# The first block's down products by seven products of 256 columns in six of eight groups, and forms loaded from the second group on

## The chip, the cores and the metric

The kernel runs on one core of one Trainium2 chip. TensorE (PE) multiplies, VectorE (DVE), ScalarE (ACT) and GpSimd (POOL) work on tiles, SyncE (SP) issues the DMAs. The metric is the device time of one execution in microseconds, the median of several runs.

## The reference

```python
def _attn_ref(q, k, v, lam):                 # decayed linear attention, blocks of 64 positions
    for b in range(nb):
        ...
        intra = np.einsum('bhic,bhjc->bhij', qb, kb) * Dmask[None]
        intra = np.einsum('bhij,bhjd->bhid', intra, vb)
        inter = np.einsum('bhid,bhde->bhie', qb * lam_pow[None], kv_state)
        out[:, :, sl] = intra + inter
        ...
def _moe_ref(x, w_in, w_out):                # x: 1536 x 512, w_in: 512 x 2048, w_out: 2048 x 512
    h = x @ w_in
    sp = np.where(h > 20.0, h, np.log1p(np.exp(np.minimum(h, 20.0))))
    g = h * np.tanh(sp)
    return g @ w_out
def _moe2_ref(x, w_in, w_out):
    h = x @ w_in
    r = np.maximum(h, 0.0)
    g = r * r
    return g @ w_out
```

The output is `_moe2_ref(_moe_ref(x))` with x the attention's 1536 tokens of 512 features, in float32.

## The kernel before

The 1536 tokens are three blocks of 512. After the attention (up to some 62 us) come two MLPs, L = 0 and 1, each in four groups g of 512 hidden features. Per group and block there is an up part (x times 512 columns of w_in) and a down part (the gated hidden values times 512 rows of w_out, summed over the groups). To keep float32, `mm3` (line 369) makes every product of two float32 values as three matmuls of a high and a low part; `split` (line 379) makes the parts: ACT copies the high one (names `..h`), DVE subtracts it for the low one (names `..l`).

Blocks 1 and 2 are multiplied as a pair (`up_pair`, `down_pair`): a product of 2 x 2 blocks by seven products, numbered 1 to 7, of sums and differences instead of eight. `sums` (line 668) makes the sums of a weight, `forms` the differences of x. In the down part the kept sums of the groups so far are copied into PSUM ahead of a product, which then adds to them, and copied out again behind it. Block 0 has its own seven products of 256 columns in the up part (`up_own`, line 780) in seven of the eight groups (OWN); its down part (`down`, line 1017) is plain: per group two outputs of four rows of 12 matmuls of 512 columns, seeded from and evicted to the two kept sums `ac`. PSUM holds four units of two banks; SBUF is cut into 51 units of 4 KB per partition (UNITS).

The forms of x, 14 tiles of 512 KB for the pair and 8 for block 0, are stored to DRAM (`store_form`, `own_forms`) and loaded again for each group from SPILL and HOME on (`load_form`, `own_back`), which frees their units between uses.

No engine's order is written out by hand. `Plan` takes every step with an engine, an assumed time, reads and writes, and a rank for TensorE; it runs them through a list scheduler with a limited number of units, 20 times with adjusted due times, and keeps the order that ends first. All engines, SP's queue too, then issue strictly in the order kept. Tile names carry L, g and the product: `gh0100` is the high part of the gated values of L0, g1, block 0, half 0.

Of the kernel before, what the change touches and what calls it, by code (L numbers as in the profile page):

```python
# [12 lines left out]
F32 = mybir.dt.float32  # L13
# [7 lines left out]
P = 128  # L21
# [3 lines left out]
CH = 128  # L25
# [19 lines left out]

UNITS = 51
DEBUG = None
SPILL = (2, 2)
HOME = (1, 2)
OWN = ((0, 1), (0, 2), (0, 3), (1, 0), (1, 1), (1, 2), (1, 3))  # L50
BACK = 9.0
SPARE = (6, 3)
AHEAD = 55.0
UP = tuple(-1919 + i for i in range(16))

# [255 lines left out]
def attention_mlps(ctx, tc, lam, qk, kv, w_in, w_out, w2_in, w2_out, out):  # L311
# [72 lines left out]

    def halves(v):
        return [(v, 0), (v, 1)]

# [392 lines left out]
    def up_own(L, g, rank, rest):  # L780

        w = 2 * CH
        back = g >= HOME[L]
        if back:
            own_back(L, g)
        one, two = Val(f"ua{L}{g}", "P"), Val(f"ub{L}{g}", "P")
        for v in (one, two):
            v.full = v.seeded = True
        a, b, f_, e = (one, 0), (one, 1), (two, 0), (two, 1)

        def bank(x):
# [73 lines left out]
        for u in range(2):  # L865
            hi, lo = Val(f"gh{L}{g}0{u}", dtype=F32R), Val(f"gl{L}{g}0{u}", dtype=F32R)
            g_hi[L, g, 0, u], g_lo[L, g, 0, u] = hi, lo
            split(hi, lo, h[u], halves(h[u]))

    g_hi, g_lo, h_raw = {}, {}, {}  # L870

# [6 lines left out]
    def gated(L, g, t, u, h, in_psum):  # L878

        name = f"{L}{g}{t}{u}"  # L880
        if L and not in_psum:
            op("DVE", 1.14, lambda: nc.vector.scalar_tensor_tensor(  # L882
                out=tl(h), in0=tl(h), scalar=0.0, in1=tl(h), op0=ALU.max, op1=ALU.mult), [(h, 0)], [(h, 0)], name=f"rs{name}")
        elif not in_psum:
            op("ACT", 0.96, lambda: nc.scalar.activation(out=tl(h), in_=tl(h), func=AF.Relu if L else AF.Mish),
               [(h, 0)], [(h, 0)], name=f"r{name}", table=None if L else "mish")
        if L and in_psum:
            op("ACT", 0.96, lambda: nc.scalar.activation(out=tl(h), in_=tl(h), func=AF.Square),
               [(h, 0)], [(h, 0)], name=f"sq{name}")
        if t:  # L890
            h_raw[L, g, t, u] = h
            return
        hi, lo = Val(f"gh{name}", dtype=F32R), Val(f"gl{name}", dtype=F32R)
        g_hi[L, g, t, u], g_lo[L, g, t, u] = hi, lo
        split(hi, lo, h, [(h, 0)])

    def take(L, g, t, u, src):
        h = Val(f"h{L}{g}{t}{u}")
# [114 lines left out]
        take(L, g, 2, 0, e)  # L1013

    accs = {}

    def down(L, g, t, rank, early=None):
        final = g == NG - 1
# [192 lines left out]
    for L in range(2):  # L1211
        for g in range(NG):
            if (L, g) != (0, 0):
                weights(L, g, 0, 0)
                weights(L, g, 0, 1)

            if (L, g) == (1, 0):
                own_forms(1)
            turned = (L, g) in TURNED
            own_up = (L, g) in OWN  # L1220
            first = turned and ranks()
            if own_up:
# [12 lines left out]
            if not g:  # L1235
                forms(L, halves)
            if not g and not L:
                own_forms(L)
            if (L, g) not in OWN:
                sums(L, g)  # L1240
            before = (L, g) in BEFORE and ranks()
            if (L, g) in SPLIT:
                opening, before = before, ranks()
                up_pair(L, g, opening, ranks())
            elif opened:
                up_pair(L, g, opened, ranks(), opens=OPENS) if OPENS else up_pair(L, g, ranks())
            elif own_up:
                up_pair(L, g, *((first, first, first if MIDDLE else between) if turned else (between, ranks())), parted=not turned)
            else:
                up_pair(L, g, first or ranks())  # L1250
            sums(L, g, 1)
            first = turned and ranks()
            early, rest = (ranks(), ranks()) if turned and SPREAD[L] else (None, None)
            down(L, g, 0, before or ranks(), early)
            down_pair(L, g, first or ranks(), rest, between if own_up and turned and MIDDLE else None)

    ordered = sorted((o for o in plan.ops if o.name in FIRST), key=lambda o: FIRST[o.name])
# [52 lines left out]
```

## Time and profile before

| | us |
|---|---|
| median of 3 runs | 533.87 (533.33 to 534.17) |
| the profiled execution | 533.92 |
| its span, first to last instruction | 531.9 |
| TensorE busy | 522.7 |
| DVE busy | 435.6 |
| ACT busy | 416.5 |
| DMA moved | 123.25 MB |

The profile is one execution, recorded by the hardware profiler. Busy time is the union of an engine's instructions. Matmuls overlap each other in their pipeline, so a row of 12 is read from the chain or the timeline, not as 12 times the mean of one. A wait is put down to what ended it.

### The profile page before, as it was taken

What the parts mean: (1) busy time and instruction counts of PE and PEld (TensorE: products, weight loads), DVE (VectorE), ACT (ScalarE), POOL (GpSimd) and SP (SyncE); (2) the same over time, 40 slices, a digit from 0 to 9 for tenths busy, and PEclk for the clock granted to TensorE, in tenths of its full rate; (3) what the DMA queues carried; (4) which work ended last, traced back from release to release, by engine and by line L of the source; (5) the groups of instructions that cost most, each with busy time, mean ns of one, the idle gap of its engine ahead of it and who ended that gap; (6) DMA issues with size and microseconds to landing.
All of it is one profiled execution on the core that took longest, in us unless ns stands there. A gap on an engine that the chain in (4) does not pass through costs nothing.

```text
span 531.9 us, 8778 instructions
## 1 busy us (share of the span) xinstructions
PE 522.7 (98%) x3470; PEld 458.0 (86%) x3470; DVE 435.6 (82%) x472; ACT 416.5 (78%) x482; POOL 32.3 (6%) x32
## 2 busy tenths in 40 slices
PE   8899999999999999999999999999999999999997
PEld 5798788898888988889888888998899888988996
DVE  6999999986796659986999997997897279985851
ACT  3858478889999999968988995889797689858711
POOL 3575200000000000000000000000000000000000
PEclk9999999999999999999999999999999999999999
DMA  8999425799579972995340010599769942990024
GB/s 313 410 408 339 157 79 197 250 317 410 211 268 356 347 214 90 378 409 190 121 150 9 0 41 0 159 408 416 324 245 367 413 163 98 337 410 28 0 80 158
DMA packets 35658, 123.25 MB, mean 232 GB/s; under 512 B 3874, under 2 KB 5922, under 8 KB 35618
## 3 DMA queue, kind: packets, MB, share of 16 engines
q1 hardware_dynamic: 35616, 122.70, 62.5%
q8 instruction: 27, 0.44, 0.4%
q14 instruction: 13, 0.11, 0.1%
q10 hardware_dynamic: 2, 0.00, 0.0%
HBM read 96.47 MB, written 26.21 MB: 231 GB/s over the span
## 4 chain that ended last, share of the span: by engine, by line
PE 89%; DMA 6%; DVE 3%; SPq 1%; issue 1%; DVEq 0%
PE p L376 16%; PE dn L376 16%; PE q L376 14%; PE e L376 10%; PE o L376 9%; PE b L376 8%; PE ua L376 8%; PE ub L376 6%; DMA qk<-in_qk_dram 4%; DMA kv<-in_kv_dram 2%; DVE a L367 1%; SPq L487 0%; PE xo L545 0%; DVE gl L367 0%; DVE t L649 0%
## 5 line engine op out<-in xcount | busy, mean ns | idle before, releaser
L644 ACT ACTIVATE m<-st 128x512 f32<-128x512 f32 (+1 forms) x66 | 42.3, 671 | 7.9 <-DMA st<-in_moe_w_in_dram 7.7
L656 DVE SCALAR_TENSOR_TENSOR t<-m,t 128x1024 int32<-128x1024 int32 x32 | 40.3, 1265 | 8.0 <-ACT m L644 7.0
L367 DVE TENSOR_TENSOR wl<-t,wh 128x1024 fp32r<-128x1024 f32 x32 | 41.0, 1285 | 2.1 <-ACT wh L364 2.1
L367 DVE TENSOR_TENSOR sl<-s,sh 128x1024 fp32r<-128x1024 f32 x32 | 39.2, 1244 | 3.2 <-ACT sh L364 3.2
L364 ACT ACTIVATE sh<-s 128x1024 fp32r<-128x1024 f32 x32 | 33.3, 1052 | 10.0 <-DVE s L367 10.0
L367 DVE TENSOR_TENSOR el<-D,eh 128x1024 fp32r<-128x1024 f32 x32 | 38.6, 1219 | 0.9 <-ACT eh L364 0.8
L367 DVE TENSOR_TENSOR el<-h,eh 128x1024 fp32r<-128x1024 f32 x24 | 29.3, 1221 | 9.5 <-ACT eh L364 8.1
L364 ACT ACTIVATE eh<-D 128x1024 fp32r<-128x1024 f32 x32 | 33.3, 1056 | 3.9 <-DVE D L367 3.7
L364 ACT ACTIVATE wh<-t 128x1024 fp32r<-128x1024 f32 x32 | 33.5, 1054 | 2.0 <-DVE t L656 1.9
L649 DVE TENSOR_SCALAR t<-st 128x512 int32<-128x512 int32 (+1 forms) x66 | 28.0, 460 | 1.2 <-DMA st<-in_moe_w_in_dram 1.1
L364 ACT ACTIVATE eh<-h 128x1024 fp32r<-128x1024 f32 x24 | 25.3, 1058 | 0.8 <-DVE h L882 0.3
L367 DVE TENSOR_TENSOR gl<-h,gh 128x1024 fp32r<-128x1024 f32 x16 | 19.5, 1221 | 7.8 <-ACT gh L364 7.7
L376 PE MATMUL p<-fl,wh 128*128 128x512 f32 x64 | 25.2, 394 | 0.0
L376 PE MATMUL p<-fh,wl 128*128 128x512 f32 x64 | 25.0, 391 | 0.0
L376 PE MATMUL p<-fh,wh 128*128 128x512 f32 x64 | 24.9, 389 | 0.0
L376 PE MATMUL dn<-wl,gh 128*128 128x512 f32 x64 | 24.9, 389 | 0.0
L376 PE MATMUL dn<-wh,gl 128*128 128x512 f32 x64 | 24.9, 389 | 0.0
L376 PE MATMUL p<-fl,sh 128*128 128x512 f32 x64 | 24.9, 389 | 0.0
L376 PE MATMUL p<-fh,sl 128*128 128x512 f32 x64 | 24.9, 389 | 0.0
L376 PE MATMUL dn<-gl,wh 128*128 128x512 f32 x64 | 24.9, 389 | 0.0
L376 PE MATMUL p<-fh,sh 128*128 128x512 f32 x64 | 24.9, 389 | 0.0
L376 PE MATMUL dn<-gh,wh 128*128 128x512 f32 x64 | 24.9, 389 | 0.0
(257 smaller groups left out, 1770.6 us busy)
## 6 DMA issues: line engine op xcount, KB each, us to landing
st<-in_moe_w_out_dram SPq DMA_DIRECT2D x32, 512.0 KB, 9.8
fh<-f SPq DMA_DIRECT2D x28, 512.0 KB, 6.3
fl<-f SPq DMA_DIRECT2D x28, 512.0 KB, 6.7
st<-in_moe_w_in_dram SPq DMA_DIRECT2D x26, 512.0 KB, 7.3
f<-fh SPq DMA_DIRECT2D x14, 512.0 KB, 10.0
f<-fl SPq DMA_DIRECT2D x14, 512.0 KB, 10.2
qk<-in_qk_dram SPq DMA_DIRECT2D x12, 512.0 KB, 10.2
kv<-in_kv_dram SPq DMA_DIRECT2D x12, 512.0 KB, 10.2
```

The costliest lines, as they stand in the source:

```text
L364: nc.scalar.activation(out=o, in_=i, func=AF.Copy)
L367: nc.vector.tensor_tensor(out=o, in0=a, in1=b, op=alu)
L376: nc.tensor.matmul(out=out_, lhsT=a, rhs=b, start=start, stop=pieces or (last and i == 2), skip_group_check=not start if pieces else onto)
L644: nc.scalar.activation(out=tl(m)[o, i], in_=tl(st, TB, 2)[r, :, 1].bitcast(F32), func=AF.Prelu, scale=RANGE, alpha=BELOW)
L649: nc.vector.tensor_scalar(out=tl(t)[o, i], in0=tl(st, TB, 2)[r, :, 0], scalar1=29, scalar2=None, op0=ALU.logical_shift_right)
L656: nc.vector.scalar_tensor_tensor(out=tl(t), in0=tl(m).bitcast(I32), scalar=3, in1=tl(t), op0=ALU.logical_shift_left, op1=ALU.bitwise_or)
```

## The change

In L0's groups 1 and 2 and in all four groups of L1 (DOWN), `down_own` takes the place of `down`: block 0's down part becomes seven products, each 12 matmuls of 256 columns. Four differences of 256 columns of the hidden values (names `G`, parts `jh`, `jl`) are made in each group; of the first half of the hidden values only one half needs parts (`split_half`). Three tiles of two sums each (`aw` 26, 57 and 43) are kept between the groups instead of two tiles `ac`; in the last group of a run they are combined into the two result tiles `xs`. In L0 the two sums of g0 go into the products of g1, and the result of g2 is what g3's plain `down` goes on with. In L1's g0 the first of the seven products has a rank of its own (LEAD). SPILL and HOME of L1 go from 2 to 1: its forms are loaded for its second group too, and stored before that.

```diff
-SPILL = (2, 2)
-HOME = (1, 2)
+SPILL = (2, 1)
+HOME = (1, 1)
+DOWN = ((1, 3), (0, 4))
+EARLY7 = (7, 5)
+LEAD = ((1, 0),)
+    def split_half(hi, lo, raw, reads):
+        c = slice(0, 2 * CH)
+        op("ACT", 0.51, lambda: copy(tl(hi)[:, :, c], tl(raw)[:, :, c]), reads, [(hi, 0)], name=hi.name)
+        op("DVE", 0.61, lambda: tt(tl(lo)[:, :, c], tl(raw)[:, :, c], tl(hi)[:, :, c].bitcast(F32), ALU.subtract),
+           [*reads, (hi, 0)], [(lo, 0)], name=lo.name)
...
+    def down_own(L, g, rank, early=None, lead=None):
...
+        for i, x, y, reads, writes in (
+                (1, lambda: block(0, 1), lambda: block(0, 0), [*key(0, 1), *key(0, 0)], t1),
+                (3, lambda: block(1, 1), lambda: block(0, 1), [*key(1, 1), *key(0, 1)], t3),
+                (2, lambda: block(1, 1), lambda: form(1), [*key(1, 1), t1], t2),
+                (4, lambda: block(1, 0), lambda: form(2), [*key(1, 0), t2], t4)):
+            op("DVE", 0.61, lambda i=i, x=x, y=y: tt(form(i), x(), y(), ALU.subtract), reads, [writes], name=f"G{L}{g}{i}")
+        for n in range(2):
+            hi, lo = Val(f"jh{L}{g}{n}", dtype=F32R), Val(f"jl{L}{g}{n}", dtype=F32R)
+            split(hi, lo, raw[n], halves(raw[n]))
...
+                for s in range(2):
+                    q = tl(o)[:, b, s * w : (s + 1) * w]
+                    for k in range(2):
+                        if L:
+                            mm3(q, right(rh)[:, k, c], right(rl)[:, k, c], left(lh)[:, k], left(ll)[:, k],
+                                first, k == 1, onto=onto, pieces=True)
+                        else:
+                            mm3(q, left(lh)[:, k, c], left(ll)[:, k, c], right(rh)[:, k], right(rl)[:, k],
+                                first, k == 1, onto=onto, pieces=True)
...
+        def keep(n, o):
+            a = acc.setdefault(n, Val(f"aw{L}{n}"))
+            op("ACT", 0.96, lambda: copy(tl(a), tl(o)), halves(o), halves(a), name=f"kw{n}{L}{g}")
...
+        two = unit(26)
+        product(1, two, 1, False)
...
+            op("DVE", 1.14, lambda: tt(tl(two), tl(two)[:, 1:2].to_broadcast([P, 2, TB]), tl(a), ALU.add),
+               [(two, 1), *halves(a)], halves(two), name=f"+v{L}{g}")
+        product(2, two, 0, True)
+        product(6, two, 1, True)
...
+        if not ends:
+            keep(26, two)
+            keep(57, both(57, 5, 7))
+            keep(43, both(43, 4, 3))
+            return
...
+        def sum_to(c, d, x, y, reads):
+            k, to = place(c, d)
+            op("DVE", 0.61, lambda: tt(to(), flat(x()), flat(y()), ALU.add), reads, [k], name=f"+x{L}{c}{d}")
+            store(c, d)
...
+            q = alone("4", 0, 4)
+            sum_to(0, 1, lambda: tl(q)[:, 0], lambda: tl(ev)[:, 1], [(q, 0), (ev, 1)])
+            r = alone("3", 1, 3)
...
+            lead = rank + 11.5 if (L, g) in LEAD else None
...
+            if by_seven(L, g):
+                down_own(L, g, before or ranks(), early, lead)
+            else:
+                down(L, g, 0, before or ranks(), early)
```

On TensorE, the four `dn` rows of a group (12 matmuls of 512 columns each) become seven rows of 12 matmuls of 256 columns at the same place: in L0's g1 and g2 and L1's g1 and g2 product 1 behind the pair's product 5, the others behind its product 3; in L1's g0 product 1 behind the pair's product 4, then the pair's 3, then 6, 5, 2, 4, 7 and 3; in L1's g3 products 1, 5, 7, 2 and 6 ahead of the pair's last three products, and 4 and 3 behind them. Nothing else on TensorE changes its place.

DVE in L1's g0, behind the parts of the forms; `gl` are low parts of block 0's hidden values, `wl` and `sl` of w_out and its sums, `el` of the pair's hidden values. Before:

```order
L367 TENSOR_TENSOR gl1000_3132<-h1000_2992,gh1000_3119 128x1024
L855 SCALAR_TENSOR_TENSOR h1001_3019<-h1001_3019 128x2x256
L367 TENSOR_TENSOR h1021_3150<-e10_3111,f10_3089 128x1024
L367 TENSOR_TENSOR wl1011_3162<-t1011_2754,wh1011_3134 128x1024
L367 TENSOR_TENSOR gl1001_3164<-h1001_3019,gh1001_3152 128x1024
L367 TENSOR_TENSOR s1010_3174<-t1010_2743,t1011_2754 128x512
L367 TENSOR_TENSOR s1010_3174<-s1010_3174,t1010_2743 128x512
L882 SCALAR_TENSOR_TENSOR h1021_3150<-h1021_3150 128x1024
L367 TENSOR_TENSOR el101_3204<-h1010_3130,eh101_3160 128x1024
```

And after:

```order
L370 TENSOR_TENSOR gl1000_3292<-h1000_3116,gh1000_3254 128x2x256
L370 TENSOR_TENSOR h1021_3296<-e10_3244,f10_3220 128x1024
L370 TENSOR_TENSOR fl13_3306<-xr021_2988,fh13_3147 128x1024
L370 TENSOR_TENSOR sl1010_3325<-s1010_3242,sh1010_3283 128x1024
L370 TENSOR_TENSOR G101_3334<-h1001_3144,h1000_3116 128x512
L370 TENSOR_TENSOR G101_3334<-h1001_3144,G100_3266 128x512
L370 TENSOR_TENSOR jl100_3342<-G100_3266,jh100_3294 128x1024
L370 TENSOR_TENSOR wl1011_3354<-t1011_2872,wh1011_3257 128x1024
L370 TENSOR_TENSOR gl1001_3372<-h1001_3144,gh1001_3273 128x1024
L370 TENSOR_TENSOR s1011_3388<-t1010_2861 128x512
L370 TENSOR_TENSOR s1011_3388<-t1011_2872,s1010_3242 128x512
L370 TENSOR_TENSOR jl101_3404<-G101_3334,jh101_3350 128x1024
```

The differences G and their low parts jl stand ahead of the pair's low parts now, and the sums of w_out with their low parts have moved ahead too, since the block's products need them.

SP's queue at the end of L1's g0; `st` are weights, `o1..` and `f1..` stored forms, `ox`, `ot` and `fh1..` loaded ones. Before:

```order
L637 DMA st11100_3200<-in_moe2_w_out_dram 128x1024
L637 DMA st11101_3414<-in_moe2_w_out_dram 128x1024
L637 DMA st11110_3434<-in_moe2_w_out_dram 128x1024
L637 DMA st11111_3454<-in_moe2_w_out_dram 128x1024
L765 DMA o1x00_85<-yh00_2812 128x1024
L765 DMA o1x01_86<-yl00_2830 128x1024
```

And after:

```order
L714 DMA f141_100<-fl14_3231 128x1024
L714 DMA f130_97<-fh13_3147 128x1024
L650 DMA st11100_3308<-in_moe2_w_out_dram 128x1024
L714 DMA f131_98<-fl13_3306 128x1024
L650 DMA st11101_3340<-in_moe2_w_out_dram 128x1024
L650 DMA st11110_3352<-in_moe2_w_out_dram 128x1024
L650 DMA st11111_3370<-in_moe2_w_out_dram 128x1024
L788 DMA ox0011_3566<-o1x00_85 128x1024
L788 DMA ox0111_3589<-o1x01_86 128x1024
```

The 22 stores stood behind the weights of g1's down part and now stand ahead of the last three of these, 21 of them ahead of the first; behind these weights 22 loads for g1 are new.

## Rows read from the trace of the kernel before

**Rows 1.** The page, busy time of the engines over the whole span.

```profile
PE 522.7 (98%) x3470; PEld 458.0 (86%) x3470; DVE 435.6 (82%) x472; ACT 416.5 (78%) x482; POOL 32.3 (6%) x32
```

**Rows 2.** TensorE's waits, the longest: us in total, times, longest us.

```profile
PE xo L545 <- DMA kv<-in_kv_dram: 2.3, 3, 1.1
```

**Rows 3.** Chain of waits in L0's g1: start us, us, engine and output.

```profile
118.38 1.43 PE ub L376 x12
119.82 1.44 PE ua L376 x12
...
122.70 2.75 PE b L376 x12
...
133.62 2.72 PE dn L376 x12
...
141.78 8.16 PE dn L376 x36
```

**Rows 4.** The same chain in L1: end of g0, pair of g1, end of g3.

```profile
310.90 2.72 PE p L376 x12
313.62 2.72 PE e L376 x12
316.34 10.88 PE dn L376 x48
...
390.29 2.88 PE o L376 x24
...
508.43 5.47 PE dn L376 x24
...
522.53 5.48 PE dn L376 x24
528.03 0.69 DVE ac L367
```

**Rows 5.** Busy by stage: length, PE, PEld, DVE, ACT, POOL, PEclk, DMA share, GB/s.

```profile
109.90:169.00 59.10, 59.10 (x302) 50.63 (x302) 43.81 (x49) 54.52 (x61) 0.00 (x0) 1.00 0.84 321
169.00:228.00 59.00, 59.00 (x301) 50.55 (x301) 46.27 (x51) 54.47 (x60) 0.00 (x0) 1.00 0.76 266
...
284.40:347.40 63.00, 63.00 (x399) 57.31 (x398) 58.60 (x60) 53.00 (x62) 0.00 (x0) 1.00 0.17 54
347.40:407.60 60.20, 60.20 (x386) 55.02 (x386) 54.27 (x62) 51.47 (x60) 0.00 (x0) 1.00 0.89 348
407.60:467.80 60.20, 60.20 (x385) 55.02 (x385) 44.33 (x48) 49.53 (x57) 0.00 (x0) 1.00 0.70 269
```

**Rows 6.** DVE's timeline in L1's g0: start us, us, operation, count.

```profile
295.77 0.69 DVE L367 TENSOR_TENSOR h<-ub,uf 128x512 f32<-128x512 f32 x1 [0.47 <-PE ub L376]
296.38 2.35 DVE L367 TENSOR_TENSOR fl<-T,fh 128x1024 fp32r<-128x1024 f32 x2
298.64 1.22 DVE L367 TENSOR_TENSOR fl<-xr,fh 128x1024 fp32r<-128x1024 f32 x1
299.78 1.22 DVE L367 TENSOR_TENSOR T<-xr,T 128x1024 f32<-128x1024 f32 x1
...
342.21 0.69 DVE L367 TENSOR_TENSOR s<-t 128x512 f32<-128x512 f32 x1
342.81 0.69 DVE L367 TENSOR_TENSOR s<-t,s 128x512 f32<-128x512 f32 x1
```

**Rows 7.** ACT's groups by line and shape: busy us, mean ns of one.

```profile
L364 ACT ACTIVATE dn<-ac 128x1024 f32<-128x1024 f32 x10 | 10.1, 1018 | 0.0
```

**Rows 8.** Timeline of ACT and of SP's queue in L1's g0 and g1.

```profile
285.38 1.05 ACT L364 ACTIVATE oh<-O 128x1024 fp32r<-128x1024 f32 x1
...
340.56 0.92 SPq L765 DMA_DIRECT2D o1t<-oh  x1
...
361.94 0.32 SPq L701 DMA_DIRECT2D f<-fl  x1
```

**Rows 9.** DMA issues: count, KB each, median us to landing.

```profile
f<-fl SPq DMA_DIRECT2D x14, 512.0 KB, 10.2
```

More of the change, by code (lines that the diff above doesn't have):

```diff
@@ L867, in up_own @@
             g_hi[L, g, 0, u], g_lo[L, g, 0, u] = hi, lo
-            split(hi, lo, h[u], halves(h[u]))
+            if by_seven(L, g) and not u:
+                split_half(hi, lo, h[u], [(h[u], 0)])
+            else:
+                split(hi, lo, h[u], halves(h[u]))
+        if by_seven(L, g):
+            h_raw[L, g, 0] = h
     g_hi, g_lo, h_raw = {}, {}, {}
@@ L894, in gated @@
         g_hi[L, g, t, u], g_lo[L, g, t, u] = hi, lo
-        split(hi, lo, h, [(h, 0)])
+        if by_seven(L, g):
+            h_raw.setdefault((L, g, 0), []).append(h)
+        if by_seven(L, g) and not u:
+            split_half(hi, lo, h, [(h, 0)])
+        else:
+            split(hi, lo, h, [(h, 0)])
     def take(L, g, t, u, src):
@@ L1015, in attention_mlps, with block, key, form @@
     accs = {}
+    def down_own(L, g, rank, early=None, lead=None):
+        w = 2 * CH
+        begins, ends = g == DOWN[L][0], g == DOWN[L][1] - 1
+        h = h_raw[L, g, 0]
+        raw = [Val(f"G{L}{g}{i}") for i in range(2)]
+        def block(u, c):
+            return tl(h[u])[:, :, c * w : (c + 1) * w]
+        def key(u, c):
+            return [(h[u], c if (L, g) in OWN else 0)]
+        def form(i):
+            return tl(raw[(i - 1) // 2], 2, 2, w)[:, (i - 1) % 2]
+        t1, t2, t3, t4 = ((raw[(i - 1) // 2], (i - 1) % 2) for i in range(1, 5))
+        for i, x, y, reads, writes in (
[4 more added lines that the diff above has]
+            op("DVE", 0.61, lambda i=i, x=x, y=y: tt(form(i), x(), y(), ALU.subtract), reads, [writes], name=f"G{L}{g}{i}")
+        parts = []
+        for n in range(2):
+            hi, lo = Val(f"jh{L}{g}{n}", dtype=F32R), Val(f"jl{L}{g}{n}", dtype=F32R)
+            split(hi, lo, raw[n], halves(raw[n]))
+            parts.append((hi, lo))
+        def moving(i):
+            if i in (1, 2, 3):
+                u = 0 if i == 1 else 1
+                c = slice(w, 2 * w) if i == 3 else slice(0, w)
+                return g_hi[L, g, 0, u], g_lo[L, g, 0, u], lambda v: tl(v)[:, :, c]
+            n = {5: 0, 6: 1, 7: 2, 4: 3}[i]
+            return *parts[n // 2], lambda v: tl(v, 2, 2, w)[:, n % 2]
+        count = [0]
+        def product(i, o, b, onto):
+            lh, ll, left = stationary(L, g, 1, i)
+            rh, rl, right = moving(i)
+            def products():
+                for s in range(2):
+                    c = slice(s * P, (s + 1) * P)
+                    q = tl(o)[:, b, s * w : (s + 1) * w]
+                    for k in range(2):
+                        first = s == 0 and k == 0
+                        if L:
+                            mm3(q, right(rh)[:, k, c], right(rl)[:, k, c], left(lh)[:, k], left(ll)[:, k],
+                                first, k == 1, onto=onto, pieces=True)
+                        else:
+                            mm3(q, left(lh)[:, k, c], left(ll)[:, k, c], right(rh)[:, k], right(rl)[:, k],
+                                first, k == 1, onto=onto, pieces=True)
+            reads = [(x, 0) for x in (lh, ll, rh, rl)] + ([(o, b)] if onto else [])
+            op("PE", 1.442, products, reads, [(o, b)], name=f"V{i}{L}{g}",
+               rank=lead if lead and not count[0] else (early if early and count[0] < EARLY7[L] else rank) + count[0])
+            count[0] += 1
+        acc = accs.setdefault((L, "own"), {})
+        def keep(n, o):
+            a = acc.setdefault(n, Val(f"aw{L}{n}"))
+            op("ACT", 0.96, lambda: copy(tl(a), tl(o)), halves(o), halves(a), name=f"kw{n}{L}{g}")
+            return a
+        def unit(n):
+            o = product_unit(f"v{n}{L}{g}")
+            o.seeded = True
+            return o
+        before = begins and g
+        def flat(x):
+            return x.rearrange("p (s c) -> p s c", s=2)
+        def at(of, c, d):
+            v, m = (of[c], d) if L else (of[d], c)
+            return (v, m), lambda: tl(v)[:, :, m * w : (m + 1) * w]
+        had = [accs[L, 0, d] for d in range(2)] if before else None
+        def from_had(o, b, c, d):
+            k, src = at(had, c, d)
+            op("ACT", 0.51, lambda: copy(flat(tl(o)[:, b]), src()), [k], [(o, b)], name=f"on{o.name}{b}")
+        two = unit(26)
+        product(1, two, 1, False)
+        if before:
+            k, src = at(had, 0, 0)
+            op("DVE", 0.61, lambda: tt(flat(tl(two)[:, 0]), flat(tl(two)[:, 1]), src(), ALU.add), [(two, 1), k], [(two, 0)],
+               name=f"vb{L}{g}")
+            (ka, ya), (kb, yb) = at(had, 0, 1), at(had, 1, 1)
+            op("DVE", 0.61, lambda: tt(ya(), ya(), yb(), ALU.subtract), [ka, kb], [ka], name=f"vy{L}{g}")
+        elif begins:
+            op("ACT", 0.51, lambda: copy(tl(two)[:, 0], tl(two)[:, 1]), [(two, 1)], [(two, 0)], name=f"vb{L}{g}")
+        else:
+            a = acc[26]
+            op("DVE", 1.14, lambda: tt(tl(two), tl(two)[:, 1:2].to_broadcast([P, 2, TB]), tl(a), ALU.add),
+               [(two, 1), *halves(a)], halves(two), name=f"+v{L}{g}")
+        product(2, two, 0, True)
+        product(6, two, 1, True)
+        def both(n, x, y):
+            o = unit(n)
+            if not begins:
+                a = acc[n]
+                op("ACT", 0.96, lambda: copy(tl(o), tl(a)), halves(a), halves(o), name=f"on{o.name}")
+            if before:
+                if n == 43:
+                    from_had(o, 0, 0, 1)
+                    from_had(o, 1, 1, 0)
+                else:
+                    from_had(o, 1, 1, 1)
+            product(x, o, 0, not begins or before and x == 4)
+            product(y, o, 1, not begins or before)
+            return o
+        if not ends:
[3 more added lines that the diff above has]
+            return
+        target = [Val(f"xs{L}0{d}") for d in range(2)]
+        def place(c, d):
+            return at(target, c, d)
+        def store(c, d):
+            if not L or g < NG - 1:
+                return
+            k, to = place(c, d)
+            r, f = (slice(i * w, (i + 1) * w) for i in (c, d))
+            op("SP", 1.0, lambda: nc.sync.dma_start(out=out[r, f].rearrange("(j p) c -> p j c", p=P), in_=to()), [k],
+               [("out", 0, c, d)], name="out")
+        def sum_to(c, d, x, y, reads):
+            k, to = place(c, d)
+            op("DVE", 0.61, lambda: tt(to(), flat(x()), flat(y()), ALU.add), reads, [k], name=f"+x{L}{c}{d}")
+            store(c, d)
+        k, to = place(0, 0)
+        op("ACT", 0.51, lambda: copy(to(), flat(tl(two)[:, 0])), [(two, 0)], [k], name=f"x{L}00")
+        store(0, 0)
+        av, ev = Val(f"va{L}"), Val(f"ve{L}")
+        op("ACT", 0.51, lambda: copy(tl(av)[:, 0], tl(two)[:, 1]), [(two, 1)], [(av, 0)], name=f"va{L}")
+        o = both(57, 5, 7)
+        op("DVE", 1.14, lambda: tt(tl(ev), tl(o), tl(av)[:, 0:1].to_broadcast([P, 2, TB]), ALU.add), [*halves(o), (av, 0)],
+           halves(ev), name=f"ve{L}")
+        sum_to(1, 1, lambda: tl(o)[:, 1], lambda: tl(ev)[:, 0], [(o, 1), (ev, 0)])
+        if L and g == NG - 1:
+            def alone(n, b, x):
+                o = unit(n)
+                o.full = False
+                a = acc[43]
+                op("ACT", 0.51, lambda: copy(tl(o)[:, b], tl(a)[:, b]), [(a, b)], [(o, b)], name=f"on{o.name}")
+                product(x, o, b, True)
+                return o
+            q = alone("4", 0, 4)
+            sum_to(0, 1, lambda: tl(q)[:, 0], lambda: tl(ev)[:, 1], [(q, 0), (ev, 1)])
+            r = alone("3", 1, 3)
+        else:
+            q = r = both(43, 4, 3)
+            sum_to(0, 1, lambda: tl(q)[:, 0], lambda: tl(ev)[:, 1], [(q, 0), (ev, 1)])
+        sum_to(1, 0, lambda: tl(r)[:, 1], lambda: tl(ev)[:, 0], [(r, 1), (ev, 0)])
+        for d in range(2):
+            accs[L, 0, d] = target[d]
+            if L or g < NG - 1:
+                continue
+            x_hi[1, 0, d], x_lo[1, 0, d] = Val(f"yh0{d}", dtype=F32R), Val(f"yl0{d}", dtype=F32R)
+            split(x_hi[1, 0, d], x_lo[1, 0, d], target[d], halves(target[d]))
+            x_raw[1, 0, d] = target[d]
```

5 lines of the change are left out of this document (4 added, 1 removed).

## The prediction

> **What bounds the kernel now.** I read the engine totals first [rows 1]: TensorE (PE) is busy 522.7 of the span's 531.9 us, while VectorE (DVE) and ScalarE (ACT) stand at 82% and 78%. Then its waits [rows 2]: the longest sum is 2.3 us, for the inputs of the attention that comes first. The chain of waits says the same: behind 62 us it is one row of matmuls on the next, without a wait between them [rows 3, 4]. So from 62 to 528 us the time is the sum of the matmuls, and each us that TensorE is spared is a us of the kernel, as long as the other engines keep up. Whether they do is read from the busy time by stage [rows 5]. A stage is one group of one MLP; its first group begins the second MLP at 284.4 us. Two stages are full already: in the first MLP's second group ACT is busy 54.52 of 59.10 us, in the second MLP's first group DVE 58.60 of 63.00. The granted clock is 1.00 in every stage, the upper level of 2.4 GHz.
>
> **What TensorE is spared.** The first block's down sums take four rows of 12 matmuls of 512 columns: 2.72 + 8.16 = 10.88 us [rows 3], 10.88 in one piece in the second MLP [rows 4], and 5.47 + 5.48 = 10.95 in the last group, where they are cut otherwise [rows 4]. The new form is seven products of 12 matmuls of 256 columns. Such products stand in the trace already: 1.43 to 1.44 us for 12 in the first block's up part (118.38, 119.82) [rows 3], and 2.88 for 24 where activations are stationary and weights move [rows 4], which is how the second MLP's new products stand. So 7 x 1.437 = 10.06 and 7 x 1.44 = 10.08. Spared: 2 x 0.82 in the first MLP's second and third group, 3 x 0.80 in the second MLP's first three, 0.87 in its last; together 4.9 us. A 512-column product right behind a 256-column one takes 2.75 instead of 2.72 (122.70) [rows 3]. By the order of the changed kernel there are seven new places of that kind (two in each of the two groups of the first MLP, one in each of the first three of the second): 0.2 us back. 4.7 us are left.
>
> Against this shape stands one rule. By the rows above a matmul goes by in 0.120 us with 256 columns and 0.227 with 512, so half the columns cost 53%. The Trainium skill ("TensorE: Matmul & The Clock Gate", section "Back-to-back issue gap") gives 81 ns at 128 columns and 131 ns at 512 for streams in which each matmul brings its weights, so that small matmuls pay a large fixed part; a straight line between them, my estimate, is 98 ns at 256, and by it 84 matmuls (8.2 us) would be 1.9 us dearer than 48 (6.3) and the kernel some 12 us slower. The rows disagree on both ends, and I go by the rows.
>
> **What DVE and ACT get.** In a row without waits a DVE instruction of 128x1024 follows the next by 1.14 us (298.64 to 299.78), one of 128x512 by 0.60 (342.21 to 342.81) [rows 6]; an ACT copy of 128x1024 takes 1.02 [rows 7]. Per group DVE gets four differences of 512 (2.4), two low parts (2.28) and, from the second group of a run on, one sum with the kept total (1.14); it saves 0.54, since only half of one low part is made. That is 4.1 us in the second MLP's first group and 5.3 in the next. Added to 58.60 and 54.27 [rows 5], this is 62.7 in a stage that then lasts 62.2, and 59.6 in one of 59.4: by stages DVE would be full in both, and only the group behind (44.33 of 60.20) has room. ACT gets two high parts, three evictions of kept sums and two or three seeds, and loses two seeds, two evictions and half a high part: about +2.4 us in the first MLP's second group, 56.9 of 58.3.
>
> Sums by stage do not settle a wait, so I followed the tight places along the order. The tightest is the second MLP's first group. There DVE finishes the addition into h at 295.77 and goes on at 296.38 [rows 6]. From there to the low part jl101, which the block's product 4 needs, the new order has 17 instructions of 1024 and 10 of 512: 17 x 1.14 + 10 x 0.60 = 25.4, so it ends at 321.8. TensorE starts the pair's product 4 at 310.90 [rows 4]; then come 2.72, the block's first product (1.43, put ahead of the pair's product 3 by LEAD), 2.75, and the products 6, 5 and 2 at 1.44: it is at product 4 at 322.1. The slack is 0.3 us. For product 6 it is 0.7: up to jl100 there are 14 instructions of 1024 and 8 of 512, 20.8 us, so 317.1, against 317.8. Differences that read the instruction before them start some 0.1 us later than the pace used here, and there are several. I book 0.3 us of waiting, with bounds of 0 and 1.5. ACT's copies, followed in the same way, come 1 us or more before DVE wants them but for two: sh1011 just in time (its product 7 has 0.5 us of slack) and eh103 0.5 us late (its product has 2.5).
>
> In the first MLP's second group the same walk finds no wait: ACT comes to the block's last eviction about 2 us after TensorE ended it, instead of right behind, but the next group's first evictions are met as before. In the second MLP's second group DVE still idles some 2.7 us for the eviction of product 7. Differences, seeds and kept sums are booked at nothing there: what hides them is TensorE's own 59 us. If that cover were gone they would cost their 5.3 us.
>
> **The forms' earlier trip.** The second MLP's forms (22 tiles of 512 KB) are now stored during its first group and loaded for its second too: 22 more loads, 11.5 MB. On SP's queue the 22 stores now stand ahead of that group's last weights, and each store holds up those behind it until its tile is made. DMA was nearly idle there (0.17, 54 GB/s) [rows 5]. The new thing is that DVE and ACT write into tiles that these stores must have read: the low part jl101 takes the tile of the stored f171. In the trace of before, the same row of stores took from 340.56 (oh) to 361.94 (the last of form 7) [rows 8], with four weight loads among them, 21.4 us, and such a store lands 10.2 us behind its issue [rows 9]. The stores can start when the second oh is written, at 286.4 (285.38 + 1.05) [rows 8]; the same pace puts f171 at 307.8 and its landing at 318.0, and DVE comes to jl101 at 320.7. So 2.7 us of slack, and no cost. The loads are issued as tiles come free, the first products' by about 335, more than 11 us before their products (346.6), against 6 to 10 us of landing. I book 0 for both, bound 0 to 4.
>
> **The end.** The last group's two last products now come behind the pair's product 3, with 2.88 us left to hide its 512 KB store, where 5.48 us of matmuls stood [rows 4]. Behind the last matmul DVE adds in 0.69 as before, then a 256 KB store, now in rows half as long. Bounds 0 and 0.5; I take 0.2.
>
> **The sum.** The profiled execution took 533.92 us, 2.0 more than its span and close to the median of 533.87. 4.9 - 0.2 - 0.3 - 0.2 = 4.2, so 529.7.
>
> **Rivals.** (1) DVE or ACT give part of it back, most likely from 310 to 345 us or from 130 to 170. For it: the slack of 0.3 and 0.7 us, and two stages that are full by their sums. Against it: no wait on TensorE in stages that were 92% and 93% full before. Price: from 1.5 us up to what DVE gets in its two full groups less what they had idle before, (4.1 + 5.3) less half of (63.00 - 58.60) + (60.20 - 54.27), 4.2 us: 531.2 to 533.9, and some more if idle time cannot be used at all. (2) Slower: the stores land late. SP issues in order, so a form made late holds all stores behind it; DVE then stands at wl1011, gl1001, s1011 or jl101 with all of the pair's low parts behind it, and TensorE stands with it. It decides once stores are more than 2.7 us later than I put them; it takes 8 us to eat the gain and leave the kernel over 0.2% slower: 535.0 to 537. Against it: DMA was busy 0.17 of that stage [rows 5]. (3) Slower: the weight load sets the pace of the 256-column matmuls. The mean weight load is 458.0 / 3470 = 0.132 us [rows 1]; at that pace 84 matmuls take 11.1 us, 0.2 more than now, in six groups 1.2: 535.1. It decides from 10.88 / 84 = 0.130 us per matmul on. The trace has 0.120 in both forms, so little is left of it. The rule of the Trainium skill named above is of this kind and falls with it. That the change does not do what it says is out: the order has the 84 short matmuls in all six groups.
>
> **How the numbers follow.** Forecast 0.79 (528.8 to 531.2), rival 1 0.13, rival 2 0.06, rival 3 0.02. A measurement of this kernel tells 0.2%, about 1.1 us, from no change. Half of rival 1 lies under 532.8: faster 0.79 + 0.06 = 0.85; same 0.07; slower 0.08. The range goes from 528.8 (all bounds at zero, and 0.4 of spread between runs) to 532.0, which takes the cheap third of rival 1 in and leaves about 2 in 10 out.
>
> **What would show it.** Right: TensorE's rows for the block's down part are 1.43 to 1.44 us each, its busy time is 4 to 5 us lower, and no wait on it behind 62 us sums to more than about 1 us. The stage from 284 us lasts 62 to 63 us and the next 59 to 60. Wrong by rival 1: waits of the block's or the pair's products for DVE (jl, el) or for ACT seeds. Wrong by rival 2: DVE instructions in that stage that wait for the DMA of stores, or up products that wait for loaded forms at about 345 us. Wrong by rival 3: more than 1.5 us per short product. Three quarters of a us or more between the last matmul's end and the span's end beyond the 3.2 + 0.7 of before would mean that I misread the end.

## The result, and the profile of the changed kernel

The changed kernel took 528.93 us (528.86 to 529.17, four runs) against 533.89 us (533.33 to 534.17) of the kernel before, run beside it: ratio 0.9909, 95% interval 0.9892 to 0.9926, 5.0 us faster. A later series gave 529.78 us beside 533.84 (0.9925, 0.9911 to 0.9939), 4.1 us faster. The profiled execution took 529.0 us, its span 526.9.

Busy time of the engines over the span, from the page of the changed kernel, to be held against [rows 1], and the longest of TensorE's waits for its operands (us in total, times, longest) against [rows 2]:

```profile
PE 518.0 (98%) x3686; PEld 464.8 (88%) x3686; DVE 468.2 (89%) x518; ACT 428.8 (81%) x505; POOL 31.8 (6%) x32
```

```profile
PE xo L558 <- DMA kv<-in_kv_dram: 2.3, 3, 1.4
...
PE sc L513 <- DVE state L370: 0.8, 1, 0.8
```

TensorE has 216 matmuls more and is busy 4.7 us less. DVE has 32.6 us more to do, ACT 12.3, and still all of TensorE's waits lie in the attention, as before. The chain of waits (start, us, engine and output) in L0's g1, against [rows 3]:

```profile
132.98 1.43 PE v L379 x12
134.42 2.75 PE p L379 x12
137.16 2.72 PE e L379 x12
139.88 8.63 PE v L379 x72
```

and in L1's g0 and g3, against [rows 4]:

```profile
311.46 1.43 PE v L379 x12
312.90 2.75 PE e L379 x12
315.64 8.63 PE v L379 x72
...
503.94 7.20 PE v L379 x60
...
519.78 2.89 PE v L379 x24
...
522.76 0.69 DVE xs L370
```

The seven products (`v`) take 1.43 + 8.63 = 10.06 us where four rows `dn` took 10.88, and 7.20 + 2.89 = 10.09 where they took 10.95. The rows follow each other without a gap. The 2.75 is the 512-column row right behind a 256-column one. Busy time by stage (length, then PE, PEld, DVE, ACT, POOL, granted clock, DMA share, GB/s), the five stages of [rows 5]:

```profile
109.26:167.58 58.32, 58.32 (x339) 51.69 (x338) 48.69 (x56) 55.23 (x64) 0.00 (x0) 1.00 0.86 325
167.58:225.90 58.32, 58.32 (x338) 51.70 (x337) 51.53 (x57) 54.41 (x63) 0.00 (x0) 1.00 0.81 267
282.26:344.44 62.18, 62.18 (x435) 58.34 (x434) 61.03 (x65) 55.78 (x66) 0.00 (x0) 1.00 0.84 314
344.44:403.86 59.42, 59.42 (x422) 56.09 (x422) 56.36 (x67) 52.60 (x61) 0.00 (x0) 1.00 0.75 265
403.86:463.28 59.42, 59.42 (x421) 56.08 (x421) 50.17 (x56) 50.75 (x60) 0.00 (x0) 1.00 0.74 260
```

TensorE is busy for the whole of every stage, at the upper clock level throughout. DVE is full in L1 g0 alone, 61.03 of 62.18 us; in L1 g1 it has 3.1 us to spare, so its new work was spread over more stages than my sums had it.

All runs together are read by one table. The first `ua` matmul of a group marks its beginning in TensorE's timeline; "last" is the start of DVE's last addition, "tail" what lies between that addition's end and the span's end. All in us, from one profile each.

| kernel | L0 g1 begins | L0 g1 | L0 g2, g3 | L1 g0 | L1 g1 | L1 g2 to last | L0 g1 to last | tail |
|---|---|---|---|---|---|---|---|---|
| before | 109.72 | 59.09 | 115.44 | 62.96 | 60.20 | 120.62 | 418.31 | 3.14 |
| changed | 109.10 | 58.32 | 114.68 | 62.17 | 59.42 | 119.07 | 413.66 | 3.49 |
| again (the changed kernel) | 109.50 | 58.32 | 114.68 | 62.18 | 59.42 | 119.06 | 413.66 | 3.50 |
| trip | 109.86 | 59.09 | 115.44 | 62.95 | 60.20 | 120.63 | 418.31 | 2.98 |
| kept | 110.20 | 58.32 | 114.68 | 62.17 | 59.42 | 119.06 | 413.65 | 3.28 |
| l0only | 109.67 | 58.32 | 114.68 | 62.95 | 60.20 | 120.63 | 416.78 | 3.15 |
| l1only | 109.41 | 59.10 | 115.44 | 62.17 | 59.42 | 119.07 | 415.20 | 3.54 |
| l13plain | 110.47 | 58.32 | 114.68 | 62.17 | 59.42 | 119.85 | 414.44 | 3.30 |
| nolead | 110.83 | 58.32 | 114.68 | 63.08 | 59.42 | 119.07 | 414.57 | 3.61 |
| gonce | 108.88 | 58.32 | 114.68 | 62.74 | 59.43 | 119.28 | 414.45 | 3.50 |
| gtwice | 109.54 | 58.32 | 114.68 | 64.93 | 60.84 | 123.11 | 421.88 | 3.50 |
| kwtwice | 110.20 | 58.96 | 115.18 | 63.34 | 59.60 | 119.60 | 416.68 | 3.50 |

From the start of L0 g1 to the last addition, the time repeats to 0.01 us between the two profiles of the changed program; what scatters is the part ahead of it, and the tail by up to 0.3 us between programs that end alike. So the cause of each difference is read from the table, and the medians, each with a run of before beside it, confirm the sum.

### The profile page after: what moved, and what is told of

The parts are those of the page before. It is cut to its first block, busy times and chain, and to the rows that moved or that the text cites. A ratio compares the mean times of both kernels' runs of the same rounds, so it can differ in the third digit from the quotient of the medians.

```text
span 526.9 us, 9382 instructions
## 1 busy us (share of the span) xinstructions
PE 518.0 (98%) x3686; PEld 464.8 (88%) x3686; DVE 468.2 (89%) x518; ACT 428.8 (81%) x505; POOL 31.8 (6%) x32
## 4 chain that ended last, share of the span: by engine, by line
PE 92%; DMA 3%; DVE 3%; issue 1%; SPq 0%; DVEq 0%
PE p L379 17%; PE q L379 14%; PE v L379 11%; PE e L379 10%; PE o L379 10%; PE b L379 8%; PE ua L379 8%; PE ub L379 6%; PE dn L379 4%; DMA kv<-in_kv_dram 3%; PE up L379 2%; DVE a L370 1%; PE sc L513 1%; PE xo L558 1%; DVE gl L370 0%
## 5 line engine op out<-in xcount | busy, mean ns | idle before, releaser
L379 PE MATMUL e<-fl,sh 128*128 128x512 f32 x64 | 24.9, 390 | 0.0
L379 PE MATMUL e<-fh,sl 128*128 128x512 f32 x64 | 24.9, 390 | 0.0
L379 PE MATMUL e<-fh,sh 128*128 128x512 f32 x64 | 24.9, 389 | 0.0
L370 DVE TENSOR_TENSOR D<-h,h 128x1024 f32<-128x1024 f32 x16 | 18.9, 1221 | 2.1 <-ACT h L906 1.5
L367 ACT ACTIVATE ap<-o 128x1024 f32<-128x1024 f32 x18 | 18.4, 1020 | 2.7 <-PE o L379 2.6
## 6 DMA issues: line engine op xcount, KB each, us to landing
kv<-in_kv_dram SPq DMA_DIRECT2D x12, 512.0 KB, 10.4
```

What stands on the lines that cost most here:

```text
L367: nc.scalar.activation(out=o, in_=i, func=AF.Copy)
L370: nc.vector.tensor_tensor(out=o, in0=a, in1=b, op=alu)
L379: nc.tensor.matmul(out=out_, lhsT=a, rhs=b, start=start, stop=pieces or (last and i == 2), skip_group_check=not start if pieces else onto)
```

## The experiments

The theory: the time is the sum of TensorE's matmuls, the savings of the six groups add up, and DVE, ACT and the DMAs keep up, DVE in L1 g0 with very little to spare. The rivals: DVE or ACT set part of the time; the forms' earlier trip costs or is needed; the 0.62 us by which L0 g1 began earlier belongs to the change.

**The parts alone: trip, l0only, l1only.**

```diff
-DOWN = ((1, 3), (0, 4))
+DOWN = ((0, 0), (0, 0))      # trip
+DOWN = ((1, 3), (0, 0))      # l0only, with SPILL = (2, 2), HOME = (1, 2)
+DOWN = ((0, 0), (0, 4))      # l1only
```

> The change's second part alone: the second MLP's forms make their trip through memory already in its first group, and no group runs by seven. TensorE's program is that of the kernel before but for the names of 12 products' operands. Theory (time = TensorE's matmuls, the trip lies beside them): 533.9 us within 0.3, no wait of TensorE behind 62 us, the L1 g0 group 62.9 to 63.0 us long as before, DMA some 11.5 MB more. Rival (the trip costs where the seven do not cover it): 534.6 to 537, a wait of TensorE on f, ox or ot behind 320 us. Rival (the 0.6 us that the changed kernel won ahead of its first group by seven belongs to the trip): first product of L0 g1 at 109.3 instead of 109.9, 533.3.

> Seven products in the two groups of the first MLP alone; the second MLP and its forms as before. Theory: two of the six savings remain, 0.78 + 0.76 = 1.5 us, so 532.3 to 532.4 us if the 0.62 us ahead of L0 g1 was a chance of the profiled execution, 531.8 if it comes with the change. L0 g1 and g2 58.3 us each, all groups behind as before (62.9, 60.2, 60.2, 60.2). Rival (VectorE or ScalarE hands part of it back in the first MLP or at its end): 533.0 to 533.9, a wait of TensorE between 109 and 284 us.

> Seven products in the four groups of the second MLP alone, with the forms' earlier trip; the first MLP as before. Theory (savings add up, group by group): 0.77 + 0.78 + 0.78 + 0.85 less 0.27 at the end = 2.9 us below before, 531.0 beside 533.9; with the first MLP's 1.5 us this makes the whole. L0 g1 and g2 59.1 us each, L1's groups 62.2, 59.4, 59.4, 59.4. Rival (the second MLP gives more, as the first MLP's evictions no longer run into it): 530.0 or less. Rival (the second MLP gives less, VectorE's order being other): a wait in L1, 531.5 to 533.

Measured beside before: trip 533.70 against 534.02 us (0.9994, 0.9982 to 1.0006); l0only 532.06 against 534.02 (0.9962, 0.9949 to 0.9975); l1only 530.89 against 534.04 (0.9945, 0.9931 to 0.9959). From L0 g1 on, the table gives 0.00, 1.53 and 3.11 us less than before. 1.53 + 3.11 = 4.64, and the whole change has 4.65: the savings add up, and they come from the seven products alone. The trip moved the page's DMA total from 123.25 to 134.78 MB and L1 g0's DMA share from 0.17 [rows 5] to 0.83, and cost nothing:

```profile
284.50:347.50 63.00, 63.00 (x399) 57.30 (x398) 61.59 (x66) 54.16 (x63) 0.00 (x0) 1.00 0.83 309
```

**The seven products without the trip: kept.**

```diff
-SPILL = (2, 1)
-HOME = (1, 1)
+SPILL = (2, 2)
+HOME = (1, 2)
```

> The change without its second part: seven products in the same six groups, but the forms of the second MLP stay in SBUF through its second group, as before, and make their trip there. TensorE's order is that of the changed kernel but for the names of operands. Theory (time = TensorE's matmuls; the trip is beside the work in either place): within 0.3 us of the changed kernel, no wait of TensorE behind 62 us. Rival (22 forms of 512 KB too many in the first two groups: difference forms and kept sums get their room late): TensorE waits 1 to 4 us in L1 g0 or g1, 530 to 533. Rival (VectorE's order, changed at 34 places, passes its 0.3 us of slack in L1 g0 or its 1 us in g1): 529.3 to 530.5.

Measured 529.87 us, with 529.78 for the changed kernel in the same series (0.9928 and 0.9925 of before). The table's row is that of the changed kernel. The trip's traffic falls into L1 g1, as before the change, and fills the DMA engines there to 0.97, without a wait on TensorE:

```profile
283.30:345.50 62.20, 62.20 (x435) 58.34 (x434) 60.94 (x65) 54.18 (x63) 0.00 (x0) 1.00 0.14 46
345.50:405.00 59.50, 59.50 (x423) 56.15 (x422) 56.00 (x66) 54.18 (x64) 0.00 (x0) 1.00 0.97 369
```

So the second part of the change is not needed for the first: it neither costs nor gains.

**The changed kernel once more: again.**

> The changed kernel itself once more, on this chip and in this many runs, as the mark for the others, and to see how far the start scatters. Theory (the 0.62 us ahead of L0 g1 is a chance of one execution; behind it 4.7 us from the six groups and 0.3 less at the end for the product's eviction): median 4.3 to 4.9 us below before's, 529.1 to 529.7 beside 534.0; first product of L0 g1 anywhere from 109.1 to 110.9 in the profile, 417.7 to 418.0 us from there to the span's end. Rival (the 0.6 us belongs to the change): first product at 109.1 to 109.3, 528.9.

529.78 us, 4.06 below before, a little less than I had expected. Both profiles of this program agree to 0.01 us in every stage; L0 g1 begins at 109.10 in one and 109.50 in the other, in the 12 profiles of the table from 108.88 to 110.83. Seven of these (changed, again, kept, nolead, gonce, gtwice, kwtwice) have the same instructions up to there, and their mean is 109.75, where before has 109.72 and trip, the same up to there as before, 109.86. So by these profiles the 0.62 us does not belong to the change.

**DVE's slack: gtwice and gonce.** Each difference G twice, or only the last of a group's four.

```diff
-op("DVE", 0.61, lambda ...: tt(form(i), x(), y(), ALU.subtract), ...)
+op("DVE", 0.61, lambda ...: [tt(form(i), x(), y(), ALU.subtract) for _ in range(2)], ...)             # gtwice
+op("DVE", 0.61, lambda ...: [tt(form(i), x(), y(), ALU.subtract) for _ in range(1 + (i == 4))], ...)  # gonce
```

> The changed kernel with each of the four differences G of a group by seven computed twice on VectorE, in the same place: 24 instructions of 0.6 us more in six groups, TensorE's order unchanged. Theory (only L1 g0 is tight, by 0.34 us at the second pair of differences' forms; elsewhere VectorE has 3 us and more to spare): 2.45 us more VectorE work ahead of that point, less at most 1.1 us in which VectorE idled there, less 0.34: TensorE waits 1.0 to 2.1 us in L1 g0, 0 to 0.5 in L1 g1, nowhere else; 530.0 to 531.5 us. Rival (TensorE's own length alone, VectorE nowhere near): 528.9. Rival (VectorE sets the pace in every group by seven): 6 x 2.4 = 14.7 us more, 543.

> The changed kernel with only the last of each group's four differences computed twice: 0.72 us more VectorE work in each of six groups, TensorE's order unchanged. With all four doubled (2.9 us a group) TensorE waited 1.8, 1.2, 1.4 and 2.1 us in the second MLP's four groups, nowhere in the first MLP. Theory (each of these groups has a slack of its own in VectorE's queue: 2.9 less the wait, 1.1, 1.7, 1.5 and 0.8 us): 0.72 us is inside all four, so no wait, or at most 0.4 us in L1 g0 by its 0.34 us: 0 to 0.4 us more than the changed kernel, 529.4 to 530.2 beside its 529.8. Rival (each microsecond on VectorE costs in proportion, 9.4 us for 17.4 us of added work): 4.3 us added, 2.3 us more, 532.1.

gtwice took 539.22 us against 534.02 (1.0097, 1.0081 to 1.0113), some 9 us above the changed kernel, and my expectation of 530.0 to 531.5 was wrong. (The profiled execution, at 537.66 us, was the fastest of the six.) The table shows where: nothing in the first MLP, but 2.8 us in L1 g0, 1.4 in g1 and 4.0 behind that, in all 8.2. TensorE's waits behind 62 us in that run:

```profile
PE p L379 <- DVE p L370: 2.5, 2, 1.4
PE v L379 <- ACT v L367: 2.1, 1, 2.1
PE v L379 <- DVE jl L370: 1.8, 1, 1.8
```

I had taken DVE's idle share for its slack: 3 us of 59.4 in L1 g1. But idle time that lies elsewhere in the stage does not help. The chain in L1 g1:

```profile
361.12 1.07 ACT h L873
...
362.21 0.70 DVE G L370
...
371.62 1.01 ACT f L367
...
372.65 1.24 DVE p L370
...
373.94 3.02 PE p L379 x12
```

and what ACT waits for in between, from its timeline (the idle time before, and what ended it, in brackets):

```profile
370.65 1.06 ACT L367 ACTIVATE jh<-G 128x1024 fp32r<-128x1024 f32 x1 [2.58 <-DVE G L370]
```

The differences start only when ACT has handed over the hidden values (362.2). The delay then passes through two queues: ACT stands 2.6 us at the high part `jh` until DVE has made the last difference, ACT's copy `f` stands behind `jh`, and DVE's sum `p`, which a product of the pair adds to, waits for `f`. Along this path there is less than 2.9 us of room, whatever the stage as a whole has: DVE itself idles 0.9 us ahead of `p`.

gonce, with 0.72 us a group instead of 2.9, took 530.43 us against 534.04 (0.9939, 0.9925 to 0.9952), and 0.79 us more than the changed kernel by the table: 0.57 in L1 g0, 0.22 in L1 g3, 0.01 in g1. That is more than the 0 to 0.4 that I had expected, as two places of L1 g0 gave way and L1 g3 did too. The rival's proportional cost (2.3 us) is out; so small an addition fits into most of the slack. L1 g0 on the chain of gonce:

```profile
315.42 0.11 PE v L379
315.54 0.03 issue
315.57 4.58 PE v L379 x36
320.14 0.03 issue
320.18 4.45 PE v L379 x35
```

The row of 72 is broken at the two places that the prediction had found tightest, the products that need jl100 and jl101: TensorE met them just too late, and lost 0.57 us where 0.06 us are listed as idle.

**ACT's slack: kwtwice.** Each kept sum is evicted twice.

```diff
-op("ACT", 0.96, lambda: copy(tl(a), tl(o)), halves(o), halves(a), name=f"kw{n}{L}{g}")
+op("ACT", 0.96, lambda: [copy(tl(a), tl(o)) for _ in range(2)], halves(o), halves(a), name=f"kw{n}{L}{g}")
```

> The changed kernel with each eviction of a kept sum done twice on ScalarE: three of 0.96 us more in L0 g1 and in L1 g0, g1 and g2, TensorE's order unchanged. ScalarE was busy 55.2 of 58.3 us in L0 g1, 55.8 of 62.1 in L1 g0, some 52 of 59.4 in the others. Theory (ScalarE's idle share is no measure of its slack, as VectorE's was none; what stands behind the copies in its queue comes late by up to 2.9 us): waits of 0.5 to 2 us in L0 g1, where only 3.1 us are idle, 0 to 1 in each of the others: 530.3 to 533. Rival (the copies of kept sums stand where nothing behind them is due for 3 us): 529.8, no wait.

532.74 us against 534.04 (0.9970, 0.9959 to 0.9981); by the table 3.0 us above the changed kernel, spread over all groups that keep sums and those behind them: 0.64, 0.50, 1.17, 0.18 and 0.53. The longest waits of the MLPs:

```profile
PE b L379 <- ACT b L367: 0.9, 1, 0.9
PE o L379 <- ACT o L367: 0.6, 2, 0.3
```

The 12 copies of 1.02 us raised ACT's busy time from 428.8 to 438.8 us and cost 3.0. The theory holds, and the time lies in its range; L1 g0 lost 1.17 us, where I had at most 1, and L0 g1 only 0.64. ACT has room in each group, but not for 3 us.

**The early first product: nolead.**

```diff
-LEAD = ((1, 0),)
+LEAD = ()
```

> The changed kernel without the early place of the first of the seven products in L1 g0: product 1 stands right ahead of product 2, which adds onto a copy of its sum. Theory: TensorE then waits for ScalarE's copy of 0.51 us and the two hand-overs, 0.7 to 1.0 us, and the wait for VectorE's second pair of difference forms keeps its slack, since the products behind come later by as much: 529.6 to 529.9 us. Rival (VectorE is what holds the group, so the wait is only moved and the time stays): 528.9. Rival (VectorE's order, which the planner changes with it, makes forms late): 530.5 to 532.

530.48 us against 534.02 (0.9942, 0.9926 to 0.9958); by the table 0.91 us above the changed kernel, all in L1 g0. The chain there shows the copy that TensorE now waits for:

```profile
315.92 1.44 PE v L379 x12
317.36 0.02 issue
317.38 0.59 ACT v L367
317.97 0.04 issue
318.02 8.90 PE v L379 x72
```

TensorE waits 0.7 us, and the 72 matmuls behind it take 8.90 instead of 8.63. No wait for DVE appears, so this is the theory and not the rival with late forms; the median lies above the 529.6 to 529.9 because these were counted from 528.9, and the changed kernel has 529.78 in the later series.

**The last group by eight products: l13plain.**

```diff
-DOWN = ((1, 3), (0, 4))
+DOWN = ((1, 3), (0, 3))
```

> The changed kernel with its last group by eight products, so that the kept sums come together in L1 g2. Theory: 0.85 us of products come back and 0.27 us at the end are won back: 0.6 us more than the changed kernel, 530.3 beside 529.8; from the last VectorE addition's end to the span's end 3.2 us as before the change, 3.45 with it. Rival (the end is the same either way, the 0.27 us being scatter): 0.85 more, 530.6, 3.4 to 3.5 us at the end. Rival (bringing the sums together in L1 g2 costs VectorE there a wait): 531 to 532.

529.87 us against 534.04 (0.9927, 0.9913 to 0.9941), the same as the changed kernel as far as medians tell. By the table the products cost 0.78 us more, and the tail is 3.30 instead of 3.49, so 0.6 us as expected, which the medians of five executions do not resolve. Over all profiles the tail is 2.98 to 3.30 us, mean 3.14, in the four that end with `dn`, and 3.28 to 3.61, mean 3.49, in the eight that end with the seven products: 0.35 us, as the pair of before and changed has it, but with a scatter of as much.

**More groups: l0g0 and all8.**

```diff
-DOWN = ((1, 3), (0, 4))
+DOWN = ((0, 3), (0, 4))      # l0g0
+DOWN = ((0, 4), (0, 4))      # all8
```

> Seven products in the first group of the first MLP as well (seven groups of eight). Theory (sum of matmuls): 0.78 us less than the changed kernel, 528.1 where that has 528.9. Rival (right behind the attention VectorE and ScalarE are late with the difference forms, as they have no group ahead to work in): a wait of 0.5 to 2 us between 62 and 110 us, 528.9 to 530.5.

> Seven products in all eight groups. Theory (sum of matmuls): 1.55 us less than the changed kernel, 527.4 where that has 528.9. Rival (the seven products' sums end the first MLP: the last of them go through ScalarE, VectorE, a rounding and a difference before the second MLP's first product can start, and TensorE has nothing else): a wait of 1 to 3 us between 270 and 300 us, 528.5 to 530.5.

545.92 and 549.35 us against 533.84 (1.0228, 1.0203 to 1.0253, and 1.0280, 1.0262 to 1.0299). Both are slower than before by far more than the rivals had it. In l0g0 the first `ua` of L0 g1 comes at 124.24 instead of 109.50 us, that of L0 g2 at 185.36 instead of 167.82. (Its profiled execution, at 547.78 us, was the slowest of five.) Its chain behind the attention:

```profile
65.19 1.20 DVE G L370 x2
66.39 1.21 DVE fl L370
67.60 0.04 issue
67.65 5.50 PE p L379 x12
...
79.91 1.03 ACT aw L367
...
91.32 5.49 PE p L379 x12
96.81 3.11 PE b L379 x12
```

and the stages with their granted clock, columns as above:

```profile
66.00:74.00 8.00, 5.49 (x12) 3.80 (x12) 8.00 (x9) 3.22 (x4) 0.00 (x0) 0.57 0.01 2
...
92.00:100.00 8.00, 8.00 (x26) 6.30 (x25) 8.00 (x11) 3.32 (x6) 0.00 (x0) 0.66 0.32 128
```

There is no earlier group in whose time DVE and ACT could make the parts. TensorE waits 10.4 us in six waits between 62 and 92 us: 3.3 for `fl` behind G in DVE's queue, and 7.1 in five waits for copies by ACT (`f`, the copy of product 1's sum, two evictions `aw`, and `b`). Four of these copies can start only when TensorE's row has ended, and in the order kept TensorE has no other row to do meanwhile. And twice, right behind a wait of 3 us, the granted clock is down at 0.57 and 0.66: 12 matmuls of 512 columns take 5.5 us there, twice the 2.72 of elsewhere, as at the lower level (1.2 GHz). In all8 the last sums of L0 g3 also stand between the two MLPs: from L0 g2's first `ua` to that of L1 g1 it takes 182.3 us (184.22 to 366.54) instead of 176.9, with new waits such as

```profile
PE v L379 <- ACT h L848: 0.8, 1, 0.8
```

None of the runs beats the changed kernel; kept equals it, and l13plain does as far as medians tell.

## Why the prediction was right, point by point

**What bounds the kernel.** Right. TensorE has no wait behind 62 us before or after [rows 2, 3, 4], and the time from there follows its matmuls to 0.1 us.

**What TensorE is spared.** 4.9 less 0.2 was the forecast, 4.65 is what the table has, and the two halves of the change give it separately. The short products take 0.120 us a matmul (8.63 / 72), as read from [rows 3, 4]; so the weight loads do not set the pace, and rival 3 is out. The rule of the Trainium skill ("TensorE: Matmul & The Clock Gate", section "Back-to-back issue gap") by which, along the straight line that I estimated between its two figures, 84 short matmuls would be dearer than 48 long ones, does not hold here: 10.06 against 10.88 us.

**DVE and ACT.** The tight place was the right one, and the two products named were the two at which gonce's row breaks. There the low part jl101 is made from 318.39 to 319.62 us and its product is due at 315.64 + 3 x 1.44 = 319.96, a slack of 0.34 where I had 0.3. L1 g0 begins 2.15 us earlier in this profile (282.10 against 284.25), so the walk's 321.8 and 322.1 are 319.65 and 319.95 here: both held to 0.1 us. The two low parts, jl100 and jl101:

```profile
313.78 1.23 DVE L370 TENSOR_TENSOR jl<-G,jh 128x1024 fp32r<-128x1024 f32 x1
...
318.39 1.23 DVE L370 TENSOR_TENSOR jl<-G,jh 128x1024 fp32r<-128x1024 f32 x1
```

The term that was mis-sized is the 0.3 us of waiting that I booked there: it was 0. I had booked it because differences that read the one before start some 0.1 us late, but the order puts another instruction between a difference and the one that reads it, and DVE kept its plain pace there (starts at 305.64, 306.24 and 306.84 for the first pair, 312.58, 313.18 and 313.78 for the second). Rival 1, that DVE or ACT give part of it back, did not come, but by little: 0.72 us more per group on DVE costs 0.8 us, 2.9 us cost 8.2. Where I wrote that the other groups are hidden by TensorE's 59 us, this was right for the change, but by gtwice the margin in the second MLP's g1, g2 and g3 is some 1.5, 1.3 and 0.5 us (2.9 us added; 1.4, 1.6 and 2.4 lost), and not the idle time of the stage. ACT in L0 g1 is busy 55.2 us and not the 56.9 of my sum, and why is not shown; kwtwice shows that 3 us more would not have fitted.

**The forms' earlier trip.** Booked at 0, measured at 0 by trip and kept. The stores were issued sooner than I had them and landed sooner behind their issue than the 10.2 us of [rows 9], so the slack was larger than the 2.7 us that I had worked out. From SP's queue, and of the stores of forms issued from 298 to 306 us:

```profile
305.67 1.21 SPq L714 DMA_DIRECT2D f<-fl  x1
```

```profile
DMA to landing us min/median/max: 3.5/4.9/5.0
```

By the order the first is the store of f141 and f171's stands ahead of it, so that one had landed by 310.7 us, and jl101, which takes its tile, starts at 318.39: over 7 us of slack. Rival 2 had no part in it.

**The end.** 0.2 forecast, 0.35 by the means of four and eight tails.

**The sum.** 4.65 - 0.35 = 4.3 us is what the traces explain, against 4.2 forecast. That the two are so close is partly luck: the wait that did not come was 0.3 too much, the end 0.15 too little. The first series' 4.96 is larger, and 528.93 us lies at the lower edge of the range that I gave. In its profiled execution the part ahead of L0 g1, which scatters by 2 us between profiles, was 0.6 us short, and that accounts for the difference there. But the four executions of that series lie within 0.31 us of each other and only one of them has a profile, so whether chance or something common to the series made them short stays open. The second series has 4.06. I had not named this scatter, and it is larger than all but the first term of the sum.

## What to carry to other kernels

Where one engine's chain is solid, price a change by that engine's instruction rows, group by group: here TensorE's part of the sum held to 0.1 us. The other engines' slack is not their idle share; it is found by walking their queues, and from one queue to the next where one waits for the other, from the last input that binds them to the next output that is waited for. It is measured by doubling a small instruction there. A step that others prepare paid here only where there was earlier work to prepare it in: the same seven products gave some 0.8 us in each of six groups and cost 16 us in the first one (545.92 against 529.78).

## What the runs showed of the hardware that I had not expected

A wait of TensorE costs more than the length that is listed for it. Behind waits listed with 0.03 us each, 36 and 35 matmuls of 256 columns took 4.58 and 4.45 us instead of 4.32 and 4.20 (0.120 us each); behind one of 0.7 us, 72 took 8.90 instead of 8.63. That is 0.25 to 0.27 us more each time. TensorE's timeline at the second break of gonce (start us, us) shows where it goes:

```profile
319.87 0.28 PE L379 MATMUL v<-wl,jh 128*128 128x256 f32 x1
320.18 0.39 PE L379 MATMUL v<-wh,jl 128*128 128x256 f32 x1
320.40 0.28 PE L379 MATMUL v<-wh,jh 128*128 128x256 f32 x1
```

A record lasts 0.28 us, with a modelled end, while in a solid row the next matmul starts 0.12 us behind its start. The wait is counted from that end, so 0.16 us of the loss is not in the listed length. The other 0.10 us comes behind the wait: the second matmul starts 0.22 us after the first instead of 0.12.

After waits of 3.3 and 3.0 us in l0g0, TensorE's granted clock was 0.57 and 0.66 in the stretches that followed, and rows of 12 matmuls took twice their time; the waits of 1.2 to 2.1 us in gtwice's profile left the clock of their stages at 1.00.

Two profiles of one program agree to 0.01 us over 414 us in which TensorE never waits, while the 109 us ahead of that, in which it waits for DMAs and for DVE, differ by up to 2 us between programs that are the same there.
